# Maxima over partitions taken by a TensorE product instead of GpSimd, and MoE1's input scaled by the maximum of v

## The chip, the cores and the metric

The kernel runs on one NeuronCore of a Trainium2 chip. TensorE (PE) multiplies, VectorE (DVE), ScalarE (ACT) and GpSimd (POOL) work element by element, SyncE (SP) issues the transfers; each runs its own queue in order and waits on semaphores. Results of TensorE land in PSUM, all else lies in SBUF. The metric is the device time of one execution in microseconds.

## The reference

```python
def attn(q, k, v):                       # 4 x 8 heads, 1152 keys, width 64
    q_pool = q.reshape(B, H, S // 2, 2, D).mean(axis=3)        # 576 queries
    scores = (1 / np.sqrt(D)) * q_pool @ k.T
    e = np.exp(scores - scores.max(-1, keepdims=True))
    return (e / (e.sum(-1, keepdims=True) + 1e-9)) @ v

x = attn(q, k, v)                        # heads side by side: 2304 x 512
h = x @ moe_w_in                         # MoE1, 512 -> 2048
x = (h * sigmoid(h)) @ moe_w_out         # 2048 -> 512
a = x @ w1; b = x @ w2                   # MoE2, 512 -> 1024
out = ((a * b) @ w3) @ w_out             # 1024 -> 1024 -> 512
```

The weights of the two MoE layers come as 64-bit floats, q, k and v as 32-bit ones.

## The kernel before, in words

Most products run as three fp16 products. An operand is multiplied by a power of two (the scale), rounded to fp16 (`hi`, by ScalarE) and the remainder is rounded again (`lo`, by VectorE or, for MoE1's `g` and MoE2's product `a*b`, by GpSimd). `hi*hi + hi*lo + lo*hi` are then accumulated in PSUM. The scale comes from the operand's largest absolute value: VectorE reduces along each partition, GpSimd over the partitions (`allmax`, L309 and L310), and `pow2` (L301 to L307, three small VectorE instructions) makes the power of two. Such maxima are taken of each v (12, for the batch entries 1 to 3), of each MoE1 input block (9), of the weight groups (`wst` of w_in and of w_out, `ws` of w1 and w2 together) and of each MoE2 input block (6).

Attention works on a batch entry, a head pair and tiles of 128 queries. A score tile (L465) lies in one of two PSUM tiles `sc`; VectorE takes the row maxima (L502), ScalarE the exponential (L482). In batch entry 0 (`WHOLE`) the exponentials are transposed by TensorE in fp32 (L514, into `sc` as well), evacuated by ScalarE (L517), multiplied with v in fp32 (L555), and the reciprocal row sums are spread over the output by a product with a tile `dg` (L523 writes it, L562 uses it). In entries 1 to 3 they are split to fp16 (L530 and L493), transposed by DMA and multiplied with the split v (L610), and ScalarE evacuates the product with v's scale into `x32` (L620).

MoE1 runs in blocks of 256 tokens: entry b gives blocks 2b (g = 0) and 2b + 1 (g = 1), the left-over queries of all entries block 8 (`x32t`). `block_ops` takes the maximum of `x32` (L632, then GpSimd), the scales (L637 and L638), and the split to `x16` (L656 and L643), all behind the last head pair's product. Then come 8 units of 24 products with w_in (`h_unit`, L676), each with tanh, gate and split behind it, and 16 of 12 products with w_out (`x_unit`, L717). Until the attention is over, the products other than scores and transposes alternate on two PSUM tiles `mm`; later there are eight (`mm` and `mt`).

When the attention's buffers are through, w1, w2, w_out and w3 of MoE2 are loaded and converted (`job`), w1 and w2 are split with the scale of `ws` (`split16`, L886 to L905), and MoE2 multiplies them (L1119), forms w3 times w_out once (`w3o`, L1015, with one buffer `w3t` for its transposed operand) and multiplies by that (L1163).

The order on every queue comes from a planner in the kernel (`Plan.run`): each operation has an engine, a cost in microseconds, the buffers that it reads and writes, and a key. The planner simulates the engines with these costs, and of the operations ready on an engine issues the one with the lowest key. The issued order is fixed in the program. A changed cost or operation therefore moves others.

Of the kernel before, what the change touches and what calls it, by code (L numbers as in the profile page):

```python
# [27 lines left out]
LOAD_AFTER = 3.0  # L28
AFTER = {PE: 0.25, ACT: 0.2, DVE: 0.15, POOL: 0.2, SP: 0.0}
# [35 lines left out]
class Plan:  # L65
# [5 lines left out]
    def op(self, eng, cost, fn, r=(), w=(), key=0.0, land=None):  # L71
# [3 lines left out]
        o.n, o.hook = len(self.ops), None  # L75
# [39 lines left out]
    def run(self):  # L115
        cand = defaultdict(list)
        free = {e: 0.0 for e in ENGINES}
        free["CTL"] = 0.0
        order = []
# [17 lines left out]
        while any(cand.values()):  # L137
# [47 lines left out]
def kernel(  # L185
# [51 lines left out]
    ident_b = Buf(Tag(1))  # L237

# [70 lines left out]
    def allmax(dst, src):  # L309
        nc.gpsimd.partition_all_reduce(dst, src, channels=P, reduce_op=bass_isa.ReduceOp.max)  # L310

    def from_f64(dst, words, dst_b, words_b, key):
# [20 lines left out]
        op(DVE, 1.85, merge, [words_b], [dst_b], key + 0.01)  # L333
# [13 lines left out]

    kts, qts, v16s, mvs = {}, {}, {}, {}
# [14 lines left out]
    def prep_q(b, g, hp):  # L363
# [20 lines left out]
        op(DVE, 0.7 + 0.13 * g, pool, [qs], [qt], i0 - 7)  # L384

    def prep_v(b, hp):
        i0 = FIRST_T[(b, 0, hp)]
        v16, mv = attn_buf(t_v16), attn_buf(t_mv) if b >= WHOLE else None
# [41 lines left out]
        op(DVE, 1.36, top, [vs], [(mv, 0)], i0 - 4)  # L430
        op(POOL, 0.4, lambda: allmax(mv.t[:, 1:2], mv.t[:, 0:1]), [(mv, 0)], [(mv, 1)], i0 - 3.9)
        op(DVE, 0.8, scales, [(mv, 1)], [(mv, 2)], i0 - 2)
        op(ACT, 1.26, hi, [vs, (mv, 2)], [(v16, 0)], i0 - 1)
        op(DVE, 1.45, lo, [vs, (mv, 2), (v16, 0)], [(v16, 1)], i0 + 0.5)
# [11 lines left out]
    def tile_ops(i):  # L446
# [53 lines left out]
        op(PE, 1.14, qk, [kt, qt], [sc], i - 1.5)  # L500
# [4 lines left out]
        op(ACT, 1.43, soft_exp, [sc, (sm, 0)], [e, (sm, 1)], i - 3.0 * whole)  # L505
        op(DVE, 0.32, inverse, [(sm, 1)], [(sm, 2)], i + 0.2)
        if whole:
            st, dg = Buf(t_s), attn_buf(t_dg)
            dgs[i] = dg
# [9 lines left out]
            op(PE, 1.1, turn32, [e, ident_b], [st, (pt, (j % 2, 0))], i + 0.3)  # L519
# [13 lines left out]
        op(DVE, 1.45, lo, [e, (sm, 2), (p16, 0)], [(p16, 1)], i + 0.8)  # L533
        op(SP, 2.75, turn, [p16], [(pt, j % 2)], i + 1, land=5.2)

    def pv_whole(b, g, hp, i, last, ps, nn, mine, x32, off):
# [22 lines left out]
        def spread():  # L559
            for (a, jj), dg in inv.items():  # L560
# [3 lines left out]
                    dg.t,  # L564
# [6 lines left out]
        op(  # L571
            PE, 0.3 if last else 0.6, spread, [ident_b] + [dg for k_, dg in inv.items() if not last or k_ == (0, 0)],
# [3 lines left out]
        op(PE, 1.4 if last else 4.5, pv, [v16] + list(mine.values()), [ps, (x32, (hp, off, 0))], i + 2.5)  # L576
# [8 lines left out]
    def pv_ops(b, g, hp, i, last=False):  # L585

        v16, mv = v16s[(b, hp)], mvs[(b, hp)]
# [30 lines left out]

        def evac():
            nc.scalar.activation(x32.t[:, hp, off : off + nn], ps.t[:, :nn], AF.Copy, scale=mv.t[:, 4:5])  # L620

        op(PE, 1.2 if last else 2.95, pv, [v16] + list(mine.values()), [ps, (x32, (hp, off, 0))], i + 2.5)
        op(ACT, 0.3 if last else 0.45, evac, [ps, (mv, 2)], [(x32, (hp, off))], i - SOON)


    def block_ops(blk, i, span):

        x32, xm = x32s[blk], moe_buf(t_xm)
        x16 = moe_buf(t_x16)
# [4 lines left out]
        def scales():  # L634
            m = xm.t
            pow2(m[:, 1:2], m[:, 2:3], m[:, 3:4])
            nc.vector.tensor_scalar_mul(m[:, 3:4], m[:, 3:4], 0.5)  # L637
            nc.vector.tensor_scalar(  # L638
                m[:, 4:5], m[:, 2:3], wst[0][:, 1:2], 2.0 ** -4, op0=ALU.mult, op1=ALU.mult
            )  # L640
# [165 lines left out]
    for b in range(B):  # L806
        for g in range(2):
            for hp in range(NP):
# [9 lines left out]
                if g:  # L818
                    pv_ops(b, g, hp, i0 + 4, last=True)
# [422 lines left out]
```

## Time and profile before

| | |
|---|---|
| median of 3 runs | 1200.62 us (1199.74 to 1205.22) |
| profiled execution, its own time | 1200.74 us |
| its span, first to last instruction | 1198.7 us |
| TensorE busy | 1108.2 us (92%) |
| VectorE busy | 792.2 us (66%) |
| ScalarE busy | 663.2 us (55%) |
| GpSimd busy | 158.1 us (13%) |
| mean granted TensorE clock | 0.974 |

Busy time counts from an instruction's start to its end. It is an average over stages that differ: the first 250 us hold batch entry 0 and the conversion of MoE1's weights, up to 745 us entries 1 to 3 run with MoE1 in their gaps, up to 857 us the last MoE1 blocks, then MoE2. A wait is put down to the engine whose signal came last; "issue" is time for which the profile shows no wait.

### The profile page before, as it was taken

Reading aid. Unit: us, or ns where it says so; the run is one execution under the profiler, and the core shown is the slowest. Engines: PE = TensorE matmul, PEld = TensorE weight load, DVE = VectorE, ACT = ScalarE, POOL = GpSimd, SP = SyncE. Lnnn points to the kernel's source line nnn. Section 1 sums busy time; section 2 is a strip of 40 time slices with the busy share of each in tenths; the row PEclk is TensorE's granted clock in tenths of the full one; section 3 lists DMA queues with packets and bytes.
Section 4 is the critical chain, followed back from the end, with each engine's and each line's share of the span. In section 5 each row is a group of like instructions: output and inputs, shape, how many; then the busy total and the mean of one; then the engine's idle time right before and its main releaser. Section 6 shows DMA issues by size and latency. Waiting matters only on the chain.

```text
span 1198.7 us, 21922 instructions
## 1 busy us (share of the span) xinstructions
PE 1108.2 (92%) x8972; PEld 809.1 (67%) x8972; DVE 792.2 (66%) x1283; ACT 663.2 (55%) x986; POOL 158.1 (13%) x156
## 2 busy tenths in 40 slices
PE   3778897999999999999899999897999999999998
PEld 2445675767776767677677777786756776767666
DVE  6988898498788788797987785576977521212110
ACT  3656667567677577686686675465634322222221
POOL 0000120012012012020020020112121111111211
PEclk9978998999999999999999999898999999999999
DMA  9635344368988997989979778454334001010001
GB/s 348 211 134 184 115 140 157 115 136 169 181 182 171 218 194 166 190 174 200 199 145 200 151 123 148 147 194 137 124 123 150 1 27 54 12 42 27 10 18 27
DMA packets 294821, 163.17 MB, mean 136 GB/s; under 512 B 256064, under 2 KB 266816, under 8 KB 294720
## 3 DMA queue, kind: packets, MB, share of 16 engines
q1 hardware_dynamic: 294720, 161.77, 55.6%
q8 instruction: 70, 1.15, 0.4%
q14 instruction: 31, 0.25, 0.1%
HBM read 80.22 MB, written 9.44 MB: 75 GB/s over the span
## 4 chain that ended last, share of the span: by engine, by line
PE 51%; DVE 3%; issue 2%; DMA 1%; ACT 1%; POOL 1%; DVEq 0%; POOLq 0%; ACTq 0%
PE mt L1119 10%; PE mm L676 7%; PE mt L1163 6%; PE mm L717 5%; PE sc L465 5%; PE mm L1119 4%; PE mm L610 4%; PE mt L1015 3%; PE mt L676 3%; PE mt L717 2%; PE mm L1163 2%; DMA pt<-p 1%; PE mm L1015 0%; DVE sm L502 0%; DVE x L643 0%
## 5 line engine op out<-in xcount | busy, mean ns | idle before, releaser
L465 PE MATMUL sc<-kt,qt 64*128 64x128 f32 (+3 forms) x960 | 200.7, 534 | 29.0 <-ACT pt L517 20.9
L502 DVE TENSOR_REDUCE sm<-sc 128x1 f32<-128x1152 f32 x144 | 193.9, 1348 | 40.5 <-PE sc L465 40.2
L676 PEld LDWEIGHTS <-w 128*128 128x128 f16 x1728 | 169.7, 100 | 60.6 <-issue 35.9
L482 ACT ACTIVATE e<-sc,sm 128x1152 f32<-128x1152 f32 x144 | 175.2, 1217 | 47.9 <-DVE sm L502 42.8
L717 PEld LDWEIGHTS <-w 128*128 128x128 f16 x1728 | 164.3, 98 | 54.2 <-issue 30.9
L676 PE MATMUL mm<-x,w 128*128 128x256 f16 x1440 | 173.2, 279 | 18.6 <-DVE x L643 9.7
L493 DVE SCALAR_TENSOR_TENSOR p<-e,sm,p 128x1152 f16<-128x1152 f32 x108 | 159.5, 1484 | 29.7 <-ACT p L530 29.2
L717 PE MATMUL mm<-g,w 128*128 128x256 f16 x1440 | 169.8, 273 | 2.8 <-POOL g L701 1.9
L465 PEld LDWEIGHTS sc<-kt,qt 64*128 64x128 f32 (+1 forms) x960 | 91.8, 182 | 97.9 <-issue 57.1
L530 ACT ACTIVATE p<-e,sm 128x1152 f16<-128x1152 f32 x108 | 134.2, 1248 | 31.4 <-DMA pt<-p 10.7
L701 POOL TENSOR_TENSOR g<-t,g 128x512 f16<-128x512 f32 x72 | 94.6, 1319 | 297.8 <-ACT g L698 237.0
L1139 DVE SCALAR_TENSOR_TENSOR abf<-mt,x2m,asb 128x384 f32<-128x384 f32 x36 | 22.1, 615 | 123.9 <-PE mt L1119 123.9
L610 PE MATMUL mm<-pt,v 128*64 128x256 f16 (+1 forms) x1944 | 89.8, 250 | 5.3 <-DMA pt<-p 5.1
L610 PEld LDWEIGHTS <-v 128*64 128x64 f16 x1944 | 81.9, 112 | 13.4 <-DMA pt<-p 6.6
L1119 PEld LDWEIGHTS <-w1h 128*128 128x128 f16 x576 | 56.1, 99 | 41.5 <-issue 6.2
L1119 PEld LDWEIGHTS <-w2h 128*128 128x128 f16 x576 | 56.2, 98 | 38.0 <-issue 1.3
L1119 PE MATMUL mt<-x2h,w2h 128*128 128x384 f16 x432 | 76.1, 326 | 0.0
L1119 PE MATMUL mt<-x2h,w1h 128*128 128x384 f16 x384 | 69.4, 331 | 2.1 <-DVE x2h L1081 1.5
L514 PE MATMUL sc<-identr,e 128*128 128x128 f32 x324 | 50.1, 308 | 17.9 <-ACT e L482 17.8
L692 ACT ACTIVATE t<-mm,xm 128x512 f32<-128x512 f32 x60 | 41.1, 685 | 38.4 <-PE mm L676 35.0
L514 PEld LDWEIGHTS sc<-identr,e 128*128 128x128 f32 x324 | 41.1, 158 | 30.1 <-ACT e L482 25.2
L517 ACT COPY pt<-sc 128x1152 f32<-128x1152 f32 x36 | 40.3, 1118 | 32.1 <-PE sc L514 31.9
(131 smaller groups left out, 1336.1 us busy)
## 6 DMA issues: line engine op xcount, KB each, us to landing
v<-in_moe_w_dram SPq DMA_DIRECT2D x32, 512.0 KB, 4.2
qs<-in_q_dram SPq DMA_DIRECT2D x16, 640.0 KB, 4.8
kt<-in_k_dram SPq DMA_DIRECT2D x16, 576.0 KB, 4.6
qs<-in_q_dram SPq DMA_DIRECT2D x16, 512.0 KB, 4.5
g<-in_moe_w_in_dram SPq DMA_DIRECT2D x16, 512.0 KB, 6.1
w<-t SPq DMA_DIRECT2D x32, 256.0 KB, 3.3
stage<-in_v_dram SPq DMA_DIRECT2D x12, 576.0 KB, 4.6
x2d<-t SPq DMA_DIRECT2D x36, 128.0 KB, 2.3
```

The lines of the kernel that those rows point to most:

```text
L465: nc.tensor.matmul(sc.t[cols, bank, : (c1 - c0) * P], qt.t[rows * D : (rows + 1) * D, 4 if last else 2 * h + j - 2 * g, cols], kt.t[rows * ...
L482: nc.scalar.activation(e.t, flat(), AF.Exp, bias=sm.t[:, 0:1], accum_out=sm.t[:, 1:2])
L493: nc.vector.scalar_tensor_tensor(p16.t[:, 1], e.t, sm.t[:, 3:4], p16.t[:, 0], op0=ALU.mult, op1=ALU.subtract)
L502: DVE, 1.36, lambda: nc.vector.tensor_reduce(sm.t[:, 0:1], flat(), axis=AX.X, op=ALU.max, negate=True),
L514: nc.tensor.transpose(to[:, c * P : (c + 1) * P], e.t[:, c * P : (c + 1) * P], ident)
L530: ACT, 1.27, lambda: nc.scalar.activation(p16.t[:, 0], e.t, AF.Copy, scale=sm.t[:, 3:4]),
L610: nc.tensor.matmul(ps.t[a * D : (a + 1) * D, :nn], v16.t[:, a, KEYS[c], tv, :], rhs, start=idx == 0, stop=idx == 3 * NK - 1,)
L676: nc.tensor.matmul(ps.t[:, f % 2 * BL : (f % 2 + 1) * BL], w16[0][ct * NQ + f // 4][:, tw, (f % 4) * P : (f % 4 + 1) * P], x16.t[:, ct, tx ...
L701: nc.gpsimd.tensor_tensor(gv(1), two(g32), gv(0), op=ALU.subtract)
L717: nc.tensor.matmul(ps.t[:, :BL], w16[1][f][:, tw, ct * P : (ct + 1) * P], gs[u].t[:, f % 4, tg, :], start=f == 0 and n == 0, stop=f == NF ...
L1119: nc.tensor.matmul(ps.t[:, :TB], buf.t[:, ct, tw, f * P : (f + 1) * P], xr.t[:, ct, tx, :], start=idx == 0, stop=idx == 11,)
L1163: nc.tensor.matmul(ps.t, ab[f].t[:, ta, m * P : (m + 1) * P], w3_b.t[:, f, tb, :], start=f == 0 and n == 0, stop=f == NF2 - 1 and n == 2,)
```

## The change

`allmax` is gone. In its place `top_mm` multiplies the column of partial maxima, spread over 128 columns by a zero stride, with the identity: each PSUM row then holds all 128 maxima, and VectorE reduces them. It takes a PSUM tile of the tag `mm`. For entries 1 to 3 the attention's output is bounded by the largest |v| of the entry, so MoE1's scale comes from v's maxima (`vmx`) before the attention is done; `mv` holds all head pairs' scales. The product of probabilities and v is then split straight from PSUM (`x_hi`, `x_lo`): for g = 1 all four head pairs, for g = 0 the last one, while the first three go through `x32` as before and are split together. Blocks 0 and 1 keep the maximum of `x32`; block 8 takes the largest `vmx`, for entry 0 from the maximum of its part of `x32t`. The constant factor in x's scale goes from 0.5 to 8, that in w_in's from 2^2 to 2^-2, so their product stays. `spread` reads the reciprocal sums with a zero stride, so `dg` is not written. The planner's costs are adjusted, a change between fp32 and fp16 products costs it 0.1, and score tiles are tied to the one before and to the transpose three tiles back.

```diff
@@ planner @@
+SWITCH = 0.1
+            late = 0.0
+            if e == PE and o.mode != mode:
+                late, mode = SWITCH, o.mode
@@ maxima over partitions @@
-    def allmax(dst, src):
-        nc.gpsimd.partition_all_reduce(dst, src, channels=P, reduce_op=bass_isa.ReduceOp.max)
+    def top_mm(dst, src, r, w, key):
+        am = Buf(t_mm)
+        op(
+            PE, 0.3,
+            lambda: nc.tensor.matmul(am.t[:, :P], src().to_broadcast([P, P]), ident, start=True, stop=True),
+            [r], [am], key,
+        )
+        op(DVE, 0.22, lambda: nc.vector.reduce_max(dst(), am.t[:, :P], axis=AX.X), [am], [w], key)
@@ prep_v @@
-        op(POOL, 0.4, lambda: allmax(mv.t[:, 1:2], mv.t[:, 0:1]), [(mv, 0)], [(mv, 1)], i0 - 3.9)
+        top_mm(lambda: col(1), lambda: col(0), (mv, (hp, 0)), (mv, (hp, 1)), i0 - 3.9)
+        if hp == NP - 1:
+            xm = xms[2 * b]
+            op(
+                DVE, 0.15, lambda: nc.vector.reduce_max(vmx[:, b : b + 1], mv.t[:, 1, :], axis=AX.X),
+                [(mv, (h_, 1)) for h_ in range(NP)], [(vmx_b, b)], i0 - 1.9,
+            )
+            op(DVE, 0.8, lambda: x_scales(xm, vmx[:, b : b + 1]), [(vmx_b, b), wst_b[0]], [(xm, 2)], i0 - 1.9)
...
@@ tile_ops @@
-        op(PE, 1.14, qk, [kt, qt], [sc], i - 1.5)
+        scores = op(PE, 1.19, qk, [kt, qt], [sc], i - 1.5, mode=1)
+        if i - 3 in turns:
+            plan.link(scores, {turns[i - 3]})
+        if i:
+            plan.link(scores, {asked[i - 1]})
+        asked[i] = scores
...
-            op(
-                DVE, 0.2,
-                lambda: nc.vector.tensor_scalar(
-                    dg.t, ident[:, :D], 0.0, sm.t[:, 3:4], op0=ALU.mult, op1=ALU.add
-                ),
-                [(sm, 2), ident_b], [dg], i + 0.6,
-            )
@@ pv_ops @@
+        straight = b >= WHOLE and not last and (g == 1 or hp == NP - 1)
+        if straight:
+            def x_hi():
+                nc.scalar.activation(x16.t[:, hp, 0], ps.t[:, :nn], AF.Copy, scale=mv.t[:, 5, hp : hp + 1])
+            def x_lo():
+                nc.vector.scalar_tensor_tensor(
+                    x16.t[:, hp, 1], ps.t[:, :nn], mv.t[:, 5, hp : hp + 1], x16.t[:, hp, 0],
+                    op0=ALU.mult, op1=ALU.subtract,
+                )
...
@@ block_ops @@
-        op(DVE, 1.25, top, [x32], [(xm, 0)], i - 6)
-        op(POOL, 0.4, lambda: allmax(xm.t[:, 1:2], xm.t[:, 0:1]), [(xm, 0)], [(xm, 1)], i - 6)
+        elif not bound:
+            op(DVE, 1.25, top, [x32], [(xm, 0)], i - 6)
+            top_mm(lambda: xm.t[:, 1:2], lambda: xm.t[:, 0:1], (xm, 0), (xm, 1), i - 6)
...
@@ split16, of w1 and w2 @@
-        op(POOL, 0.4, lambda: allmax(ws2[:, 4:5], ws2[:, 0:1]), [ws2_b], [ws2_b], key)
+        top_mm(lambda: ws2[:, 4:5], lambda: ws2[:, 0:1], ws2_b, ws2_b, key)
```

The order of instructions at three places follows. First GpSimd's queue in MoE1's block 8, before the change. `g` are the gated values whose low parts GpSimd subtracts, `ws` the maximum of w1 and w2, `x2m` that of MoE2's first block.

```order
L701 TENSOR_TENSOR g_177<-t_3_187,g_177 128x2x256
L701 TENSOR_TENSOR g_177<-t_1_185,g_177 128x2x256
L701 TENSOR_TENSOR g_178<-t_0_184,g_178 128x2x256
L310 ISA
L310 ISA ws_192<-ws_192 128x1
L701 ISA
L701 TENSOR_TENSOR g_178<-t_2_186,g_178 128x2x256
L701 TENSOR_TENSOR g_179<-t_1_185,g_179 128x2x256
L701 TENSOR_TENSOR g_179<-t_0_184,g_179 128x2x256
L701 TENSOR_TENSOR g_180<-t_4_188,g_180 128x2x256
L701 TENSOR_TENSOR g_180<-t_1_185,g_180 128x2x256
```

The same units of block 8 on GpSimd after the change:

```order
L766 TENSOR_TENSOR g_174<-t_2_183,g_174 128x2x256
L766 TENSOR_TENSOR g_174<-t_3_184,g_174 128x2x256
L766 TENSOR_TENSOR g_175<-t_1_182,g_175 128x2x256
L766 TENSOR_TENSOR g_175<-t_2_183,g_175 128x2x256
L766 TENSOR_TENSOR g_176<-t_3_184,g_176 128x2x256
L766 TENSOR_TENSOR g_176<-t_1_182,g_176 128x2x256
L766 TENSOR_TENSOR g_177<-t_4_185,g_177 128x2x256
L766 TENSOR_TENSOR g_177<-t_0_181,g_177 128x2x256
```

The instructions without operands and the all-reduce between the subtractions are gone; the subtractions follow one another.

Second, TensorE's queue in the same block, at the end of the fifth unit (products with w_in tiles `w_0`), before:

```order
L676 MATMUL mm_82<-x_1_182,w_0_14_159 128x256
L676 LDWEIGHTS w_0_14_159
L676 MATMUL mm_82<-x_1_182,w_0_14_159 128x256
L676 LDWEIGHTS w_0_2_147
L676 MATMUL mm_83<-x_1_182,w_0_2_147 128x256
L676 LDWEIGHTS w_0_2_147
```

and after, where the product of `ws` with the identity stands ahead of the sixth unit:

```order
L741 MATMUL mm_84<-x_1_179,w_0_14_156 128x256
L741 LDWEIGHTS w_0_14_156
L741 MATMUL mm_84<-x_1_179,w_0_14_156 128x256
L320 MATMUL mm_83<-identr,ws_189 128x128
L741 LDWEIGHTS w_0_2_144
L741 MATMUL mt_7786<-x_1_179,w_0_2_144 128x256
```

TensorE now has in its own queue, between two units, an instruction that needs `ws` from VectorE.

Third, VectorE's queue from the last split of probabilities (`p`) to the input of block 7 (`x_0`), before, with the maxima and the scales (`xm`) of blocks 7 and 8:

```order
L493 SCALAR_TENSOR_TENSOR p_2_111<-e_108,sm_124,p_2_111 128x1152
L632 TENSOR_REDUCE xm_190<-x_0_115 128x1
L632 TENSOR_REDUCE xm_191<-x32t_116 128x1
L303 TENSOR_SCALAR xm_190<-xm_190 128x1
L304 TENSOR_SCALAR xm_190<-xm_190 128x1
L307 TENSOR_SCALAR xm_190<-xm_190 128x1
L637 TENSOR_SCALAR xm_190<-xm_190 128x1
L638 TENSOR_SCALAR xm_190<-xm_190,wst_72 128x1
```

After these come seven small ones and the two splits L643 of 1024 columns, for blocks 7 and 8. The whole place after the change:

```order
L533 TENSOR_SCALAR sm_129<-sm_129 128x1
L536 RECIPROCAL sm_129<-sm_129 128x1
L539 SCALAR_TENSOR_TENSOR p_1_111<-e_108,sm_127,p_1_111 128x1152
L539 SCALAR_TENSOR_TENSOR p_2_112<-e_109,sm_129,p_2_112 128x1152
L673 SCALAR_TENSOR_TENSOR x_0_178<-mm_84,mv_130,x_0_178 128x256
L705 SCALAR_TENSOR_TENSOR x_1_179<-x32t_117,xm_188,x_1_179 128x4x256
L760 SCALAR_TENSOR_TENSOR t_4_185<-t_0_181,mm_84 128x512
```

The maxima and the scales have left the place, and of block 7's split one head pair is left.

## Rows read from the trace of the kernel before

**Rows 1.** busy time of each engine in stretches of the span, us
```profile
30.00:205.00 175.00, 144.98 (x1035) 97.66 (x1034) 158.31 (x313) 115.72 (x168) 12.95 (x15) 0.89 0.47 158
...
253.00:745.00 492.00, 474.07 (x4811) 358.18 (x4811) 401.07 (x586) 351.74 (x483) 70.98 (x60) 0.99 0.89 175
745.00:857.00 112.00, 95.70 (x896) 83.51 (x894) 76.51 (x123) 62.92 (x120) 21.27 (x20) 0.94 0.47 143
857.00:1199.00 342.00, 334.54 (x1780) 229.40 (x1778) 109.33 (x176) 95.33 (x165) 51.54 (x53) 0.99 0.16 51
```

**Rows 2.** TensorE's waits over the span: us in total, times, longest
```profile
PE sc L465 <- ACT pt L517: 20.9, 17, 2.0
...
PE mt L717 <- POOL g L701: 9.6, 2, 8.9
...
PE mm L717 <- POOL g L701: 1.9, 1, 1.9
PE mt L1119 <- DVE x2h L1081: 1.5, 1, 1.5
```

**Rows 3.** TensorE's waits for the split input from 300 to 770 us
```profile
PE mm L676 <- ACT x L656: 7.9, 5, 3.5
PE mm L676 <- DVE x L643: 7.3, 6, 1.9
```

**Rows 4.** order of time at block 7's start: start, us, what [idle before]
```profile
754.27 0.47 ACT L620 ACTIVATE x<-mm,mv 128x256 f32<-128x256 f32 x1 [6.40 <-PE mm L610]
...
757.72 1.15 ACT L656 ACTIVATE x<-x,xm 128x1024 f16<-128x1024 f32 x1 [1.97 <-DVE xm L637]
...
758.90 1.28 DVE L643 SCALAR_TENSOR_TENSOR x<-x,xm,x 128x1024 f16<-128x1024 f32 x1 [0.15 <-ACT x L656]
758.91 0.27 PE L676 MATMUL mm<-x,w 128*128 128x256 f16 x1 [3.53 <-ACT x L656]
...
760.23 6.95 PE L676 MATMUL mm<-x,w 128*128 128x256 f16 x47 [1.05 <-DVE x L643]
```

**Rows 5.** order of time on TensorE, first units of blocks 5 and 6
```profile
595.85 4.34 PE L676 MATMUL mm<-x,w 128*128 128x256 f16 x23 [1.14 <-DVE x L643]
...
674.67 2.67 PE L676 MATMUL mm<-x,w 128*128 128x256 f16 x23 [0.76 <-DVE x L643]
```

**Rows 6.** order of time around the maximum of w1 and w2
```profile
826.18 0.38 POOL L310 PARTITION_ALL_REDUCE ws<-ws  x1 [6.15 <-issue]
...
834.59 2.26 POOL L701 TENSOR_TENSOR g<-t,g 128x512 f16<-128x512 f32 x2 [8.04 <-issue]
...
835.79 5.76 PE L717 MATMUL mt<-g,w 128*128 128x256 f16 x36 [8.89 <-POOL g L701]
```

**Rows 7.** order of time before it: first loads, TensorE's unit 4, last partial maximum
```profile
761.51 1.76 SPq L918 DMA_DIRECT2D v<-in_moe_w_dram  x4
...
814.18 5.40 PE L676 MATMUL mm<-x,w 128*128 128x256 f16 x48
...
817.25 0.19 ACT L929 ACTIVATION_READ_ACCUMULATOR wfb<-w 128x1 f32 x1
```

**Rows 8.** line L514, transposes: duration in ns, least, median, most
```profile
L514 PEld LDWEIGHTS sc<-identr,e x324: 137/142/231, 13.2 to 236.4; 128*128 128x128 f32 x162
L514 PE MATMUL sc<-identr,e x324: 272/273/476, 13.2 to 236.5; 128*128 128x128 f32 x162
```

**Rows 9.** VectorE's groups of instructions by line: busy us, mean ns, idle before
```profile
L760 DVE TENSOR_REDUCE wmx<-w 128x1 f32<-128x512 f32 x32 | 21.8, 680 | 0.5
...
L632 DVE TENSOR_REDUCE xm<-x 128x1 f32<-128x1024 f32 x8 | 9.7, 1215 | 8.9 <-ACT x L620 8.7
L523 DVE TENSOR_SCALAR dg<-identr,sm 128x64 f32<-128x64 f32 x36 | 8.7, 249 | 5.7 <-PE mm L562 5.5
...
L767 DVE TENSOR_REDUCE wst<-wmx 128x1 f32<-128x16 f32 x2 | 0.3, 164 | 0.0
```

**Rows 10.** busy time of each engine from 861 to 892 us
```profile
861.00:892.00 31.00, 31.00 (x186) 19.48 (x185) 27.97 (x41) 12.81 (x24) 6.17 (x5) 1.00 0.50 164
```

More of the change, by code (lines that the diff above doesn't have):

```diff
@@ L152, in run @@
             o.start = at
+            late = 0.0
+            if e == PE and o.mode != mode:
+                late, mode = SWITCH, o.mode
             if e != "CTL":
-                free[e] = at + o.cost
-            o.end = at + (o.cost if o.land is None else o.land)
+                free[e] = at + o.cost + late
+            o.end = at + (o.cost if o.land is None else o.land) + late
             order.append(o)
@@ L570, in pv_whole @@
         sp, rs = Buf(t_mm), attn_buf(t_rs)
-        op(
-            PE, 0.3 if last else 0.6, spread, [ident_b] + [dg for k_, dg in inv.items() if not last or k_ == (0, 0)],
+        first = op(
+            PE, 0.3 if last else 0.6, spread, [ident_b] + [(dg, 2) for k_, dg in inv.items() if not last or k_ == (0, 0)],
             [sp, (rs, 0)], i + 1.0,
@@ L575, in pv_whole @@
         op(ACT, 0.3 if last else 0.45, lambda: nc.scalar.copy(rs.t[:, :nn], sp.t[:, :nn]), [sp], [(rs, 1)], i - SOON)
-        op(PE, 1.4 if last else 4.5, pv, [v16] + list(mine.values()), [ps, (x32, (hp, off, 0))], i + 2.5)
+        pv_op = op(PE, 1.1 if last else 4.4, pv, [v16] + list(mine.values()), [ps, (x32, (hp, off, 0))], i + 2.5, mode=2)
+        plan.link(pv_op, {first})
         op(
@@ L619, in evac @@
         def evac():
-            nc.scalar.activation(x32.t[:, hp, off : off + nn], ps.t[:, :nn], AF.Copy, scale=mv.t[:, 4:5])
-        op(PE, 1.2 if last else 2.95, pv, [v16] + list(mine.values()), [ps, (x32, (hp, off, 0))], i + 2.5)
-        op(ACT, 0.3 if last else 0.45, evac, [ps, (mv, 2)], [(x32, (hp, off))], i - SOON)
+            nc.scalar.activation(x32.t[:, hp, off : off + nn], ps.t[:, :nn], AF.Copy, scale=mv.t[:, 4, hp : hp + 1])
+        op(PE, 0.85 if last else 2.95, pv, [v16] + list(mine.values()), [ps, (x32, (hp, off, 0))], i + 2.5, mode=2)
@@ L626, in block_ops, with hi @@
+        op(ACT, 0.3 if last else 0.45, evac, [ps, (mv, (hp, 2))], [(x32, (hp, off))], i - SOON)
     def block_ops(blk, i, span):
-        x32, xm = x32s[blk], moe_buf(t_xm)
-        x16 = moe_buf(t_x16)
+        b, g = divmod(blk, 2)
+        bound = WHOLE <= b < B
+        x32, xm = x32s.get(blk), xms[blk]
+        x16 = x16s[blk]
+        n_ = NP - 1 if bound else NP
         def top():
             nc.vector.reduce_max(xm.t[:, 0:1], x32.t, axis=AX.XY, apply_absolute_value=True)
[L634 to L640, printed above, removed]
+        def hi():
+            nc.scalar.activation(x16.t[:, :n_, 0], x32.t[:, :n_], AF.Copy, scale=xm.t[:, 3:4])
@@ L662, in block_ops @@
+        if not (bound and g):
+            got = [(x32, (h_, 0)) for h_ in range(n_)] if bound else [x32]
+            to = [[(x16, (h_, t)) for h_ in range(n_)] for t in range(2)]
+            op(ACT, 0.15 + 0.25 * n_, hi, got + [(xm, 2)], to[0], i - 6)
+            op(DVE, 0.15 + 0.27 * n_, lo, got + [(xm, 2)] + to[0], to[1], i - 6)
         units = NF // 2 + 4 * NC
```

139 lines of the change are left out of this document (90 added, 49 removed).

## The prediction

> **What bounds the kernel now.** I read four views. First the busy time by stretches [rows 1]: from 253 to 745 us (attention of the batch entries 1 to 3 with MoE1 in its gaps) TensorE is busy 474.07 of 492 us, and from 857 us to the end (MoE2) 334.54 of 342, so there a microsecond taken from TensorE's waits is a microsecond of the end. In the first entry (30 to 205 us) it is busy only 144.98 of 175 at a mean clock of 0.89, while VectorE is busy 158.31: VectorE paces that stage. From 745 to 857 TensorE is busy 95.70 of 112 although nothing else is full: something makes it wait.
>
> Second, TensorE's waits [rows 2, 3] say what. In the first entry it waits above all for ScalarE's evacuations of transposed tiles (20.9 us). From 300 to 770 us it waits 7.9 + 7.3 = 15.2 us for `x` of L656 and L643, the split MoE1 input, at the starts of blocks 2 to 7. It also waits 9.6 + 1.9 = 11.5 us for GpSimd's low part of `g` (L701).
>
> Third, the order of time at such a start [rows 4]: block 7's input is complete at 754.74 us, its maximum is reduced by VectorE, then by GpSimd, turned into a scale by five small VectorE instructions, split by ScalarE (1.15) and by VectorE (1.28, begun 758.90). TensorE, with no scores left to fill the gap, stands 3.53 us and then 1.05. A long gap costs again behind it: block 5's first unit needed 4.34 us for 23 products, block 6's 2.67 [rows 5], which is half the granted clock, 1.2 instead of 2.4 GHz, over 1.7 us of lost time.
>
> Fourth, GpSimd at 826 us [rows 6]: the all-reduce itself takes 0.38 us, but GpSimd waits for nothing on the profile for 6.15 us before it and for 8.04 us behind it, before the next subtraction of `g`. In the order rows, instructions without operands stand at just these two places: GpSimd changes its code. TensorE stands 8.89 us for it and then runs 36 products in 5.76 us, where 48 take 5.40 at full clock [rows 7], so 5.76 - 36/48 x 5.40 = 1.7 us more.
>
> **The change part by part, against the profiled run's 1200.74 us** (its span is 1198.7, what lies around it 2.0; the median of the runs shown is 1200.62, so both bases agree).
>
> 1. *Starts of blocks 2 to 7.* With the scale known from v, the last head pair's product goes from PSUM into `x` by one ScalarE and one VectorE instruction of 256 columns (the like-sized evacuation L620 takes 0.47 [rows 4]), instead of evacuation, maximum, all-reduce, scale and two splits. TensorE has a score tile or a MoE product to run meanwhile at blocks 2 to 6, at block 7 the tail's product. Of 15.2 us I take off 14; the bounds are 8 and 15.2. Of the half-clock losses behind the starts of blocks 3, 5 and 7 (4.34 - 2.67 = 1.7 us, three times) I take off 4, bounds 0 and 5.
>
> 2. *GpSimd's code changes.* No all-reduce is left, so no change of code after the start: off go 11.5 us of TensorE's wait and the 1.7 us of clock, -13.2. Both ends of this are firm, as the subtractions then follow ScalarE directly.
>
> 3. *What is late next there.* The maximum over w1 and w2 is now a product in TensorE's own queue, behind unit 4 of block 8, and the rest of MoE1 is queued behind it. Its last partial maximum came at 817.25 + 0.19 = 817.44 us, from weights whose loads began at 761.51, when the attention's buffers were through [rows 7]. With block 8's input split without the chain, those loads start about 3 us earlier (x's last split would begin some 3 us sooner than in rows 4), so about 814.3. TensorE finished unit 4 at 814.18 + 2.7 = 816.9, half of the 48 products begun there [rows 7]; without block 7's wait (3.53 + 1.05 = 4.6) and clock loss (1.7) it is there at 810.6. So a new wait of 814.3 - 810.6, about 4 us: +4, bounds 0 (the loads gain as much as TensorE) and 8 (VectorE, whose queue holds the reduction, is late as well).
>
> 4. *The products' price.* 24 products of a column against the identity. The nearest row is the 128x128 fp32 transposes: weights 0.14 us, matmul 0.27 in the median and 0.48 at most [rows 8]. Hidden weights and pipelining give 0.14 as the low end, the slowest row 0.48; I take 0.3. Nine fall in the first entry's stage, which TensorE does not pace; 15 do count: +4.5, bounds 2 and 7. VectorE's reduction of each lies between 0.164 (16 columns) and 0.680 (512 columns) [rows 9], by the line between them 0.28, 24 times 6.7 us; it loses seven of nine maxima at 1.2 us (8.5) and 36 `dg` at 0.249 (9.0), so it has more room, not less. Each product also holds one of two PSUM tiles that the MoE units alternate on, for that reduction; score tiles, which use other PSUM, stand beside most products in the new order, so I cost it at nothing; without that cover it is one wait of up to 1 us for each of the 8 in the middle stage.
>
> 5. *First entry.* `dg` goes: 36 x 0.249 = 9.0 us of VectorE, and 5.5 us in which VectorE stood until TensorE released a `dg` buffer [rows 9]. At best the stage shortens by 14.5; at worst by nothing, as ScalarE's evacuations also end waits there [rows 2]. The scores are now tied to the transpose three tiles before; nothing in the profile prices that. I take half, -7.
>
> 6. *MoE2's beginning.* The wait of 1.5 us for `x2h` (L1081), which came behind a code change, goes [rows 2]; but the first two W3 products now stand with only the small product between them, and their one transposed operand buffer must be refilled meanwhile by four instructions of 512 columns, 0.68 us each by the nearest row [rows 9], 2.7 in a line and about 2 where ScalarE's and VectorE's overlap: +0.5 on balance, bounds -1.5 and +2.7.
>
> Sum: -14 - 4 - 13.2 + 4 + 4.5 - 7 + 0.5 = -29.2, so 1171.5; forecast **1172**.
>
> **Rivals.**
>
> *The tail gives its gain back.* From 861 to 892 us VectorE is busy 27.97 of 31 us and TensorE 31.00 [rows 10]. If TensorE arrives at MoE2 about 14 us earlier while VectorE's conversion of the weights does not, the first W3 products wait. Then block 7's start (4.6), its clock (1.7) and the GpSimd stall's 9.6 + 1.7 are lost again, less the new wait already counted (4): +13.6, so about 1186. For it: VectorE is nearly full there. Against it: from 745 to 857 us VectorE is busy only 76.51 of 112 [rows 1], part of that idleness came from the same stall, and the conversion would use it.
>
> *Slower: TensorE becomes the one that waits for maxima.* GpSimd is busy 70.98 of 492 us in the middle stage [rows 1] and could stand in its queue before each v maximum; TensorE cannot. If each of the 15 products on the path waits for the VectorE reduction before it, which itself stands behind one wide maximum and one wide split, that is 1.22 + 1.28 = 2.5 us each by the nearest rows [rows 4, 9], 37.5 us: 1172 + 37 = 1209. It decides from 29.2 / 15 = 1.9 us a product on. Against it: in the new order the v maxima of entries 2 and 3 are reduced tens of VectorE instructions ahead of most of their products; only one or two stand within ten. The Trainium skill ("GPSIMD Engine Reference", Engine selection) gives a reduction along partitions to GpSimd, which is the rule that speaks against this change. Here a row has 0.38 us for the reduction and 6.15 + 8.04 = 14.2 us of standing around it [rows 6], so the trace doesn't bear the rule out where the code must be changed.
>
> *No difference.* The starts' waits are replaced one for one: the direct splits hold a PSUM tile until VectorE, with two wide instructions ahead, has read it, and the first entry stays bound by ScalarE. Then only the GpSimd stall goes, against the products and the new wait: -13.2 + 4 + 4.5 + 0.5 = -4.2, about 1197.
>
> **How the numbers follow.** Forecast 0.68, tail rival 0.14, no difference 0.09, slower 0.09. The forecast's own bounds: best -15.2 - 5 - 13.2 + 0 + 2 - 14.5 - 1.5 = -47.4, so 1153; worst -8 - 0 - 13.2 + 8 + 7 - 0 + 2.7 = -3.5, so 1197; all bad ends together are unlikely, and the range of 8 in 10 is 1153 to 1194, which takes in the tail rival. Half a per cent, 6 us, is what a measurement of this kernel can tell from no change: faster is below 1194.6. Faster: the forecast but for 0.02, and the tail rival, and a little of the third, 0.82; same 0.10; slower 0.08.
>
> **What would show it.** After: no idle of 6 us or more on GpSimd that ends in nothing shown; no wait of TensorE for GpSimd's `g`; waits for `x` at blocks 2 to 7 under 2 us in sum; a wait of some microseconds before the product on `ws`, where I put 4; VectorE's `dg` rows gone and the first entry's last block-0 product some 7 us earlier; MoE2 as long as before. The forecast is wrong if waits at the 24 products (or for PSUM tiles behind them) exceed 10 us, if the first W3 products wait over 8 us, or if the first entry doesn't shorten.

## The result and the profile after

| | before | after |
|---|---|---|
| median | 1202.19 us (1199.74 to 1205.22, 4 runs) | 1167.12 us (1166.58 to 1168.36, 4 runs) |
| ratio | | 0.9709, 95% interval 0.9682 to 0.9735 |
| span of the profiled execution | 1198.7 us | 1164.8 us |

The forecast was 1172, between 1153 and 1194, faster with a chance of 0.82. The time came out 35 us under before, 5 us under the forecast.

Busy time by stretches, cut at the same events in both kernels (start, first unit of MoE1's block 1, first MoE2 product, end); first the kernel before. Columns: stretch, length, busy time of PE, PEld, DVE, ACT, POOL, granted clock, DMA share, GB/s.

```profile
0.00:253.30 253.30, 203.96 (x1491) 138.01 (x1492) 205.62 (x402) 153.49 (x220) 14.34 (x23) 0.93 0.51 172
253.30:857.25 603.95, 569.99 (x5706) 441.88 (x5706) 477.53 (x708) 414.51 (x603) 92.25 (x80) 0.98 0.81 169
857.25:1198.70 341.45, 334.29 (x1778) 229.18 (x1775) 109.08 (x175) 95.18 (x165) 51.54 (x53) 0.99 0.16 51
```

The same view of the kernel after:

```profile
0.00:252.40 252.40, 199.94 (x1514) 137.69 (x1515) 204.03 (x374) 155.26 (x223) 10.65 (x14) 0.91 0.53 175
252.40:825.02 572.62, 562.45 (x5721) 439.72 (x5721) 469.12 (x719) 410.60 (x598) 86.91 (x64) 1.00 0.89 179
825.02:1164.80 339.78, 333.96 (x1788) 230.10 (x1785) 107.49 (x175) 94.88 (x163) 50.08 (x48) 1.00 0.15 49
```

Nearly all of it lies in the middle: 603.95 to 572.62, 31.3 us. There TensorE's idle time fell from 34.0 to 10.2 us (length minus busy), and its busy time by 7.5 although it has ten products more, with a granted clock of 1.00 instead of 0.98 (by these two digits 0.02 x 604, about 12 us of lost clock, an estimate). The first stretch ends 0.9 us earlier, MoE2 is 1.7 us shorter.

The forecast had it otherwise: -22.7 us by its terms 1 to 4, nearly all of it in the middle, and -7 in the first entry.

TensorE's waits over the span after (us in total, times, longest):

```profile
PE sc L565 <- ACT e L528: 17.9, 5, 10.9
PE sc L511 <- ACT pt L568: 16.5, 13, 1.8
...
PE mm L658 <- DMA pt<-p: 6.0, 6, 1.8
...
PE mt L320 <- DVE x2m L1165: 2.8, 1, 2.8
...
PE mm L741 <- DVE vmx L323: 1.4, 1, 1.4
...
PE mm L741 <- DVE x L673: 0.2, 1, 0.2
```

Of the 15.2 us for `x` [rows 3] 0.2 are left, of the 11.5 for GpSimd's `g` [rows 2] nothing. The waits of the first entry are there as before. New is a wait of 2.8 us for `x2m`, the maximum of MoE2's first block.

Block 7's start after, in order of time (start, us, what [idle before]):

```profile
736.37 0.47 ACT L670 ACTIVATE x<-mm,mv 128x256 f16<-128x256 f32 x1 [4.18 <-PE mm L658]
736.88 0.48 DVE L673 SCALAR_TENSOR_TENSOR x<-mm,mv,x 128x256 f16<-128x256 f32 x1 [9.08 <-ACT x L670]
...
737.41 2.78 PE L741 MATMUL mm<-x,w 128*128 128x256 f16 x24 [0.23 <-DVE x L673]
```

Two instructions of 256 columns stand where TensorE waited 4.6 us for a chain [rows 4], and the unit behind runs at the full clock, 2.78 for 24 products.

The maximum of `ws` after, in order of time:

```profile
789.80 0.17 DVE L964 TENSOR_REDUCE ws<-wmx 128x1 f32<-128x16 f32 x1 [0.19 <-ACT wfb L1007]
789.81 2.78 PE L741 MATMUL mm<-x,w 128*128 128x256 f16 x24
...
792.43 0.39 PE L320 MATMUL mm<-identr,ws 128*128 128x128 f32 x2
```

The last partial maximum came about 28 us earlier than before (817.44, [rows 7]), while TensorE came to this place 24 us earlier. So the product found its operand there and waited for nothing. GpSimd's line after names no wait but that for ScalarE (busy, mean ns | idle before):

```profile
L766 POOL TENSOR_TENSOR g<-t,g 128x512 f16<-128x512 f32 x72 | 96.9, 1346 | 709.9 <-ACT g L763 709.9
```

### The profile page after: what moved, and what is told of

It is laid out like the page before. It is cut to its first block, busy times and chain, and to the rows that moved or that the text cites. A ratio compares the mean times of both kernels' runs of the same rounds, so it can differ in the third digit from the quotient of the medians.

```text
span 1164.8 us, 21847 instructions
## 1 busy us (share of the span) xinstructions
PE 1096.4 (94%) x9020; PEld 807.5 (69%) x9020; DVE 780.6 (67%) x1266; ACT 660.7 (57%) x983; POOL 147.6 (13%) x126
## 5 line engine op out<-in xcount | busy, mean ns | idle before, releaser
L511 PE MATMUL sc<-kt,qt 64*128 64x128 f32 (+3 forms) x960 | 197.0, 527 | 27.4 <-ACT pt L568 16.5
L782 PEld LDWEIGHTS <-w 128*128 128x128 f16 x1728 | 163.8, 98 | 42.1 <-issue 18.8
L741 PEld LDWEIGHTS <-w 128*128 128x128 f16 x1728 | 165.5, 98 | 39.5 <-issue 18.5
L782 PE MATMUL mm<-g,w 128*128 128x256 f16 x1536 | 180.4, 273 | 1.7 <-DMA w<-t 1.7
L741 PE MATMUL mm<-x,w 128*128 128x256 f16 x1416 | 163.7, 273 | 4.3 <-DVE t L760 1.8
L574 ACT ACTIVATE p<-e,sm 128x1152 f16<-128x1152 f32 x108 | 134.4, 1249 | 37.9 <-DMA pt<-p 11.8
L1217 DVE SCALAR_TENSOR_TENSOR abf<-mt,x2m,asb 128x384 f32<-128x384 f32 x37 | 22.7, 615 | 120.2 <-PE mt L1197 119.1
L658 PEld LDWEIGHTS <-v 128*64 128x64 f16 x1944 | 80.9, 111 | 13.2 <-DMA pt<-p 6.3
L1197 PE MATMUL mt<-x2h,w1h 128*128 128x384 f16 x456 | 80.4, 326 | 0.0
L565 PE MATMUL sc<-identr,e 128*128 128x128 f32 x324 | 47.7, 300 | 17.9 <-ACT e L528 17.9
L568 ACT COPY pt<-sc 128x1152 f32<-128x1152 f32 x36 | 40.0, 1116 | 26.3 <-PE sc L565 26.3
```

What stands on the lines that cost most here:

```text
L511: nc.tensor.matmul(sc.t[cols, bank, : (c1 - c0) * P], qt.t[rows * D : (rows + 1) * D, 4 if last else 2 * h + j - 2 * g, cols], kt.t[rows * ...
L565: nc.tensor.transpose(to[:, c * P : (c + 1) * P], e.t[:, c * P : (c + 1) * P], ident)
L574: ACT, 1.27, lambda: nc.scalar.activation(p16.t[:, 0], e.t, AF.Copy, scale=sm.t[:, 3:4]),
L658: nc.tensor.matmul(ps.t[a * D : (a + 1) * D, :nn], v16.t[:, a, KEYS[c], tv, :], rhs, start=idx == 0, stop=idx == 3 * NK - 1,)
L741: nc.tensor.matmul(ps.t[:, f % 2 * BL : (f % 2 + 1) * BL], w16[0][ct * NQ + f // 4][:, tw, (f % 4) * P : (f % 4 + 1) * P], x16.t[:, ct, tx ...
L782: nc.tensor.matmul(ps.t[:, :BL], w16[1][f][:, tw, ct * P : (ct + 1) * P], gs[u].t[:, f % 4, tg, :], start=f == 0 and n == 0, stop=f == NF ...
```

## The experiments

Ratios are to the kernel before on the same chip. Except where it is said, an edit is made to the kernel after, whose ratio is 0.9709 (0.9682 to 0.9735); line numbers then shift by up to ten. The kernel after has one measurement of 4 runs, so a difference to it can hold a difference of chips. The intervals of dg_back, old_plan, no_links, code_change, twice, thin_wmx and thin_evac overlap with its own: what such a run shows lies in its trace.

| run | edit | median us | ratio (95%) |
|---|---|---|---|
| pool_max | maxima back on GpSimd | 1185.29 | 0.9866 (0.9834 to 0.9899) |
| x_max | x bounded by its own maximum | 1193.45 | 0.9934 (0.9914 to 0.9954) |
| both_back | both | 1190.61 | 0.9899 (0.9864 to 0.9934) |
| no_dg | before, without `dg` | 1192.29 | 0.9925 (0.9899 to 0.9952) |
| dg_back | `dg` written again | 1170.29 | 0.9737 (0.9722 to 0.9752) |
| old_plan | planner undone | 1169.50 | 0.9731 (0.9715 to 0.9747) |
| no_links | links of score tiles out | 1166.90 | 0.9705 (0.9674 to 0.9736) |
| code_change | one all-reduce put back | 1174.46 | 0.9762 (0.9713 to 0.9812) |
| twice | every product twice | 1163.25 | 0.9675 (0.9627 to 0.9722) |
| thin_wmx | weight maxima of 32 columns | 1158.61 | 0.9638 (0.9590 to 0.9687) |
| thin_evac | half the evacuations' columns | 1168.08 | 0.9722 (0.9664 to 0.9780) |
| sum_bound | weights bounded by a sum | 1144.93 | 0.9532 (0.9493 to 0.9572) |

**pool_max.**

```diff
     def top_mm(dst, src, r, w, key):
-        am = Buf(t_mm)
-        op(PE, 0.3, ...)
-        op(DVE, 0.22, ...)
+        op(POOL, 0.4, lambda: nc.gpsimd.partition_all_reduce(dst(), src(), ...), [r], [w], key)
```

> All maxima over partitions go back to GpSimd's all-reduce, everything else stays as after the change (v still bounds MoE1's input, the planner and the links stay). Theory (two separate gains): GpSimd's changes of code return at ws, so TensorE waits again for g near the end of MoE1 (11.5 us and about 1.7 of clock in the profile before), while the 15 products that lie on TensorE's path go (0.4 us each by the rows after, 6 us): 1167 + 13.2 - 6 = 1174, between 1171 and 1180, and the starts of blocks 2 to 7 stay without a wait for x. Rival A (the products made the whole gain): 1190 to 1200. Rival B (the products cost what they save): 1163 to 1169.

Measured: 18 us more than after; the theory's 7 was too little. The stretch from block 1's first unit to MoE2 is 12.3 us longer than after (584.9 us), MoE2 4.1 us, where TensorE waits 5.3 us for `x2h`. TensorE's waits from 250 to 860 us:

```profile
PE mm L779 <- POOL g L763: 11.1, 3, 7.0
PE mt L779 <- POOL g L763: 5.4, 2, 4.0
...
PE mm L738 <- DVE x L670: 0.2, 1, 0.2
```

The starts stay free of waits, as said. But GpSimd's changes of code now stop TensorE in the middle stage too, at maxima of v; one of them on GpSimd, in order of time:

```profile
294.93 0.38 POOL L318 PARTITION_ALL_REDUCE mv<-mv  x1 [6.25 <-DVE sm L533]
303.50 1.14 POOL L763 TENSOR_TENSOR g<-t,g 128x512 f16<-128x512 f32 x1 [8.20 <-issue]
```

and TensorE there:

```profile
304.70 1.23 PE L779 MATMUL mm<-g,w 128*128 128x256 f16 x5 [6.98 <-POOL g L763]
```

**x_max.**

```diff
-        straight = b >= WHOLE and not last and (g == 1 or hp == NP - 1)
+        straight = False
-        bound = WHOLE <= b < B
+        bound = False
...
```

> MoE1's input is again bounded by its own maximum: all nine blocks take the maximum of x32, reduced by the product with the identity, and are split from x32 in one piece; v's maximum is used for v alone. The rest is as after the change. Theory (the waits at the starts of blocks 2 to 7 hang on the chain of evacuation, maximum, scale and two splits, not on GpSimd's part of it): most of the 18 us forecast for the starts (14 of idle and 4 of clock) is lost again, 1167 + 14 = 1181, between 1176 and 1187, with TensorE's waits for x of 8 us or more in sum. Rival (the all-reduce on GpSimd was the slow part of the chain, so the product alone shortens the starts): 1167 to 1173, waits for x under 5 us.

Measured: 26 us more than after, more than the theory, and by another way than it said. TensorE's waits from 250 to 860 us begin with

```profile
PE sc L511 <- ACT e L528: 10.3, 8, 3.0
PE mm L658 <- DMA pt<-p: 5.8, 5, 2.1
PE mm L741 <- DVE x L705: 2.7, 3, 1.4
```

The waits for `x` are small (the last row above and one of 1.6 us for L702): putting the chain back did not bring back the 15.2 us of before, so the theory falls. Of what was lost, 7.6 us went into waits of score tiles for exponentials, at 250 to 265 us, where MoE1's block 1 was not ready to fill the gaps (its first unit began at 272 instead of 252 us). The order was planned anew, so how much is the chain and how much the order stays open.

**both_back.** The two edits together.

> Both parts undone together, with the planner, the links and the spread without dg left as after the change: maxima on GpSimd and MoE1's input bounded by its own maximum. Alone they cost 18 us (GpSimd) and 26 us (own maximum), 44 together, while the whole change is worth 35. Theory (the two overlap: a start that waits for the chain gives GpSimd time to change its code beside it): 1196 to 1203, which leaves the rest of the change (planner, links, dg) at 0 to 6 us. Rival (they add up, and the rest of the change costs time): 1208 to 1214.

Measured: below both theories. TensorE's waits from 250 to 860 us:

```profile
PE mt L779 <- POOL g L763: 8.9, 1, 8.9
PE mm L738 <- DVE x L702: 5.9, 6, 1.4
PE mm L738 <- ACT x L699: 3.8, 1, 3.8
...
PE mm L779 <- POOL g L763: 0.2, 1, 0.2
```

The waits for `x` and the one long GpSimd stall of the kernel before are back (9.7 and 8.9 us), but the stalls in the middle stage, 11.1 us in pool_max, are 0.2 here. In these orders the product alone gave nothing (1190.6 to 1193.5), v's bound alone 5.3 us (the intervals overlap in both cases), the two together 23.5, clear of noise. That GpSimd's code changes lay beside the starts' waits fits these rows, but the order differs too, so it is not shown.

**no_dg.** The kernel before with one edit.

```diff
-                lambda: nc.vector.tensor_scalar(dg.t, ident[:, :D], 0.0, sm.t[:, 3:4], ...),
...
-                    dg.t,
+                    dg.t[:, 3:4].to_broadcast([P, D]),
```

> The kernel before with one edit alone: dg is not written, and the spread products read the reciprocal sums with a zero stride (sm with twelve buffers, as after the change). Everything else is the kernel before: GpSimd's maxima, own maximum of x, old planner. The forecast's term 5 by itself: 1201 - 7 = 1194. With both other parts undone the rest of the change was worth 10 to 12 us; if dg is all of it: 1189 to 1192. If most of that is the planner's: 1196 to 1200. Rival (the waits in the middle stage take the gain back): 1199 to 1202.

Measured: 10 us off, between 6 and 12 by the interval. Its stretches, cut as those of before and after, and then those of both_back:

```profile
0.00:243.24 243.24, 197.07 (x1491) 135.40 (x1491) 199.04 (x370) 152.72 (x220) 16.61 (x23) 0.96 0.51 177
243.24:846.70 603.46, 570.38 (x5707) 442.08 (x5707) 472.84 (x704) 414.62 (x603) 96.87 (x80) 0.98 0.81 170
846.70:1187.50 340.80, 332.62 (x1778) 228.63 (x1776) 108.99 (x175) 95.17 (x165) 51.54 (x53) 1.00 0.15 51
```

```profile
0.00:255.02 255.02, 199.30 (x1491) 138.53 (x1491) 198.99 (x370) 152.27 (x220) 13.71 (x23) 0.92 0.49 169
255.02:844.80 589.78, 566.18 (x5708) 439.28 (x5708) 475.48 (x703) 413.52 (x602) 97.41 (x80) 0.99 0.83 174
844.80:1189.50 344.70, 335.25 (x1778) 229.46 (x1775) 110.20 (x176) 95.36 (x165) 51.78 (x53) 0.99 0.15 51
```

Against before the first stretch is 10.1 us shorter and the others stay within 0.7, so the edit to `dg`, with the order planned anew, did in the first entry what term 5 said. Of the 10.1 us 6.9 are TensorE's busy time, at a mean clock of 0.96 instead of 0.93; only 3.2 are idle time. both_back differs from this kernel by the planner's part (and the buffers of v's scales) and takes nearly the same time, but by another way: 11.8 us more in the first stretch, 13.7 less in the middle, 3.9 more in MoE2. The new planner gives away in the first entry what `dg` gained there, and wins it back in the middle.

**dg_back.** The reverse of it in the kernel after.

> dg is written again by VectorE (36 instructions of about 0.25 us in the first entry, with its four buffers, and sm with its eight) and the spread products read it. The rest is as after the change. Theory from the two traces (VectorE does not pace the first entry, so dg was beside other work): 1167 to 1169. The forecast's own step (half of 14.5 us): 1174, with block 1's first unit 7 us later.

Measured: 3.2 us more. The reduction that ends entry 0 (`vmx`, L323 after) is a milestone for the first entry. In the kernel after, then here (times: first and last start):

```profile
L323 DVE TENSOR_REDUCE vmx<-mm x1: 282/282/282, 252.1 to 252.1; 128x1 f32<-128x128 f32 x1
```

```profile
L324 DVE TENSOR_REDUCE vmx<-mm x1: 280/280/280, 257.6 to 257.6; 128x1 f32<-128x128 f32 x1
```

The same line in code_change, whose first entry is that of the kernel after (its edit lies far behind):

```profile
L323 DVE TENSOR_REDUCE vmx<-mm x1: 281/281/281, 254.8 to 254.8; 128x1 f32<-128x128 f32 x1
```

So this milestone moves by 2.7 us between two traces of one order; of the 5.5 us that the first entry lost here, between 2.8 and 5.5 may be the work for `dg`. The middle is 2 us shorter than after (570.6 us), where TensorE's waits for DMA transposes are 2.9 instead of 6.0 us; in traces of the order of after they are 3.6 to 6.0 (0.4 in twice).

**old_plan and no_links.**

```diff
-SWITCH = 0.1
+SWITCH = 0.0
-        if i - 3 in turns:
-            plan.link(scores, {turns[i - 3]})
-        if i:
-            plan.link(scores, {asked[i - 1]})
...
```

no_links takes out the four lines on links alone.

> The planner's part of the change is undone: no cost for a change between fp32 and fp16 products, the old costs, and no links of the score tiles to the one before and to the transpose three back (nor of the product with v to its spread). The products and v's bound stay. Theory (that part is worth little, the forecast counted nothing for it): 1167 within 4 us either way, 1163 to 1171. Rival (a good part of the gain is the planner's, above all in the first entry): 1175 or more, with the first unit of block 1 over 5 us later than at 252.4 us.

> Only the links of the score tiles (to the one before and to the transpose three back) are taken out; the costs stay, and the order is planned anew. Theory (the links slow the first entry, where the run with the old planner was 4 to 6 us earlier, and the costs serve the rest): 1161 to 1165. Rival (the links and the costs only work together): 1167 to 1171.

Measured: 2.4 us more, and the same as after. The planner's part is worth 0 to 3 us in the end, and the theory for no_links falls: without the links entry 0 ends at 253.0 us, no earlier than after. With the old planner it ends at 246.9, 5.2 earlier, and the middle loses it again (580.1 us against 572.6). That is the same exchange as between no_dg and both_back.

**code_change.**

```diff
                 nc.gpsimd.tensor_tensor(gv(1), two(g32), gv(0), op=ALU.subtract)
+                if blk == 2 * B and u == 4:
+                    nc.gpsimd.partition_all_reduce(wst[0][:, 3:4], wst[0][:, 0:1], ...)
```

> One all-reduce of a column that nothing reads is put back on GpSimd, behind the subtraction of the fifth unit of block 8; the order on every engine is otherwise as after the change, and nothing waits for its result. Theory (GpSimd changes its code before and behind it, 6.15 and 8.04 us before the change): the subtraction of the sixth unit begins at about 812 instead of 801 us, TensorE, which wants it at 803.2, waits 10 us, 2.8 of which were a wait anyway: 1167 + 7.5, with the clock behind it up to 9.2, 1174 to 1177. Rival (the all-reduce costs its 0.4 us, the stall before the change came from ws being late): 1167 to 1168.

Measured: 7.3 us more, as the theory said. In the traces 2.7 of it lie in the first entry, which the edit does not touch; the middle is 5.6 us longer (578.2 us), which is about the stall below less the 2.8 us of the wait for `x2m` that it replaces. GpSimd in this run:

```profile
797.93 1.16 POOL L766 TENSOR_TENSOR g<-t,g 128x512 f16<-128x512 f32 x1 [2.61 <-ACT g L763]
804.62 0.90 POOL L768 PARTITION_ALL_REDUCE wst<-wst  x1 [5.53 <-ACT t L757]
812.60 3.37 POOL L766 TENSOR_TENSOR g<-t,g 128x512 f16<-128x512 f32 x3 [7.08 <-issue]
```

and TensorE:

```profile
813.79 6.41 PE L786 MATMUL mt<-g,w 128*128 128x256 f16 x41 [8.22 <-POOL g L766]
```

The operand was there since the first entry, so the 5.53 us before the all-reduce are no wait for data, whatever the row names as releaser. The instructions without operands show in the trace by name, here right behind the subtraction that ends at 799.09:

```profile
L768 POOLq MODIFY_POOL_CONFIG  x2: 12/12/12, 799.0 to 799.1; - x2
```

In the kernel before the partial maxima had been reduced when GpSimd came free there, at 820.03, 6.15 us before its all-reduce:

```profile
819.52 0.16 DVE L886 TENSOR_REDUCE ws<-wmx 128x1 f32<-128x16 f32 x1
```

So the stall of the kernel before was the change of code, not a late `ws`: that rival falls.

**twice.**

```diff
-            lambda: nc.tensor.matmul(am.t[:, :P], src().to_broadcast([P, P]), ident, start=True, stop=True),
+            lambda: [nc.tensor.matmul(am.t[:, :P], ..., ident, start=True, stop=True) for _ in range(2)],
```

> Each of the 24 products with the identity runs twice, into the same PSUM tile; the order on every engine stays as after the change. Forecast: 0.3 us each for the 15 on TensorE's path, 1167 + 4.5 = 1171.6; by the rows after, where one product takes 0.39 to 0.46 us with its two weight loads, 1167 + 6 = 1173. Rival A (they lie in TensorE's gaps): 1167 to 1168. Rival B (the slower rival of the forecast, a wait behind each): over 1180.

Measured: 3.9 us less by the medians, with intervals that overlap; no theory said so. A product's row after, and the same one here:

```profile
389.94 0.39 PE L320 MATMUL mm<-identr,mv 128*128 128x128 f32 x2
```

```profile
385.59 0.61 PE L320 MATMUL mm<-identr,mv 128*128 128x128 f32 x4
```

The second copy adds 0.22 us, so the price is between 0.22 and the 0.38 to 0.49 of a whole one, near the 0.3 of the forecast. The total is hidden by two other things: entry 0 ends 2.3 us earlier, where the mean clock from 30 to 120 us was 0.92 instead of 0.84, and the waits for DMA transposes are 0.4 instead of 6.0 us. The first is no more than two traces of one order differ (2.7 us between after and code_change, which ended later at a clock of 0.87), so it need not come from the edit or the clock; for the second no cause is shown. For the time of the whole the run is inconclusive; it rules out the rival of long waits behind each product.

**thin_wmx and thin_evac.** What paces the first entry?

```diff
-                    wmx[wi][:, c : c + 1], whole[c], axis=AX.X, ...
+                    wmx[wi][:, c : c + 1], whole[c][:, :32], axis=AX.X, ...
```

```diff
-                nc.scalar.copy(pt32(pt)[:, j % 2], st.t...[:, :S])
+                nc.scalar.copy(pt32(pt)[:, j % 2, : S if i < 8 else S // 2], st.t...[:, : S if i < 8 else S // 2])
```

> The 32 maxima of the converted MoE1 weights read 32 of their 512 columns (this leaves out most of that maximum); the order on every engine stays as after the change. This takes about 32 x (0.68 - 0.2) = 15 us of VectorE out of the first 120 us. The forecast's reading (VectorE paces the first entry): 1152 to 1160. Theory from the trace after (VectorE's work there lies beside a ring of two score tiles in PSUM, through which scores, exponentials, transposes and evacuations pass in turn): 1164 to 1167.

> From the ninth score tile of the first entry on, ScalarE evacuates 576 of the 1152 transposed columns (the rest of the tile is left as it was, so part of the computation is left out); the order on every engine stays as after the change. 28 evacuations become about 0.6 us shorter, 17 us of ScalarE, and each PSUM tile comes free 0.6 us earlier. Theory (the ring of two score tiles paces the first entry): 5 to 15 us faster, 1152 to 1162. Rival (VectorE paces it): 1165 to 1167.

Measured: 8.5 us less, and 1.0 more, which is no change. The end of entry 0 (252.1 after) in thin_wmx, then in thin_evac:

```profile
L323 DVE TENSOR_REDUCE vmx<-mm x1: 280/280/280, 246.0 to 246.0; 128x1 f32<-128x128 f32 x1
```

```profile
L323 DVE TENSOR_REDUCE vmx<-mm x1: 281/281/281, 251.0 to 251.0; 128x1 f32<-128x128 f32 x1
```

My theory of the two PSUM tiles falls: 28 evacuations of 634 instead of 1116 ns on average, 13 us of ScalarE, bring 1.1 us there, less than the 2.7 by which two traces of one order differ. 16 us less of VectorE (32 maxima of 180 instead of 680 ns) bring 6.1. The two runs were timed on the same chip, at the same mean clock from 30 to 120 us (0.91), and differ by 9.5 us in the median and 5.0 at this line. VectorE paces the stage in part, as the forecast read it.

**sum_bound**, drawn from that.

```diff
-                DVE, 0.69,
-                lambda c=c: nc.vector.reduce_max(wmx[wi][:, c : c + 1], whole[c], ...),
+                ACT, 0.9,
+                lambda c=c, junk=junk: nc.scalar.activation(junk.t, whole[c], AF.Abs, accum_out=wmx[wi][:, c : c + 1]),
...
-            [xs], [(xm, 0)], early + 1,
+            [xs], [(xm, 0)], early + 1, land=1.75 if bk else 5.0,
```

> An attempt to beat both kernels: MoE1's weights are bounded by the sum of their absolute values along each partition, which ScalarE accumulates (about 0.9 us each), instead of VectorE's 32 maxima (0.68 us each); the constant factors are shifted to match. The reduction of MoE2's first input is also given a later landing in the planner, so that its product is issued later. The order is planned anew. Theory (VectorE paces the first entry in part and ScalarE doesn't: 16 us less of VectorE gave 8.5 us, 17 us less of ScalarE gave none): 1157 to 1162, without TensorE's wait of 2.8 us for that product. Rival (ScalarE's 29 us more are paid in the same stage): 1167 or more.

Measured: 1144.9, 22 us under after and 56 under before on the same chip, more than the theory. Entry 0 ends at

```profile
L323 DVE TENSOR_REDUCE vmx<-mm x1: 282/282/282, 232.2 to 232.2; 128x1 f32<-128x128 f32 x1
```

19.9 us earlier, which the 16 us of VectorE do not explain at the rate of thin_wmx (6.1): the rest came with the new order and was not taken apart. The wait of 2.8 us for `x2m` is gone. The bound is looser than the maximum, so the split weights use less of the fp16 range.

## Why the prediction was right

*Term 1, the starts (-14 of idle, -4 of clock).* The waits went as forecast: 15.0 us of those for `x`, and the middle ran at the full clock, which gave more than the 4 + 1.7 us counted (TensorE's busy time there fell by 7.5 us with ten products more). What v's bound is worth by itself is less clear: taken back alone (x_max) it costs 26 us, but in other waits than the term named.

*Term 2, GpSimd's code changes (-13.2).* The mechanism is shown: the waits are gone, and one all-reduce put back costs 7.3 us, 5.6 of them in the stretch in which it stands. But the term counted only the stall that the trace of before showed. With the starts' chain gone, GpSimd's other maxima would have cost waits of 11.1 us more in the middle (pool_max).

*Term 3, the new wait for `ws` (+4).* Mis-sized: 0. The loads gained 28 us, TensorE 24; the term's lower bound was the case. A wait of 2.8 us came instead at the product for `x2m`, which the forecast did not name.

*Term 4, the products (+4.5).* The size is confirmed, 0.22 to 0.49 each, and VectorE's reduction takes 0.285 us where 0.28 was read off a line between two rows. No wait for a PSUM tile or a reduction of more than 2.8 us stands behind any of them, so the slower rival's price of 2.5 us each is refuted.

*Term 5, the first entry (-7).* As a saving of `dg` it holds: 10 us in the kernel before, 2.8 to 5.5 us of the first entry in the kernel after, on both sides of the 7. As a forecast of the stage it failed: block 1 begins only 0.9 us earlier in the change as a whole, and a first entry that does not shorten was one of the forecast's own signs of being wrong. The term noted the new ties of the scores and put the planner at nothing. The runs show that the planner's part costs 11.8 us in the first entry and wins 13.7 us in the middle (no_dg to both_back), or 5.2 and 7.5 (old_plan to after).

*Term 6, MoE2's beginning (+0.5).* -1.7 over all of MoE2: the wait for `x2h` went, those for `w3t` are 1.5 us.

*The sum.* By parts it holds: `dg` made -10.0 against -7, the planner's part -1.7 against nothing, the two main parts together, against both_back, -23.5 against the -22.2 of terms 1 to 4 and 6. By stages it does not: the middle gave 31.3 us instead of some 23, the first entry 0.9 instead of 7. That the total is within 5 us of the forecast rests on the planner's losses and gains cancelling, for which the working had no reason; to that extent it is luck. Nor do the two main parts add up one by one: -5.3 and +2.8 alone. The working treated each wait as a price of its own, and the total came out because the change does both. *Rivals:* the tail did not give its gain back (MoE2 is not longer), no start's wait was replaced by another; the third rival's other half, a first entry that keeps its length, did come, though not because ScalarE bounds it (thin_evac).

## What to carry to other kernels

When two waits lie in one stretch, removing one may give little: with v's bound alone the waits for GpSimd's `g` grew from 9.1 (both_back) to 16.5 us (pool_max). Test both together before dropping either. When the order is planned anew, compare stage by stage: a total that stays the same can hide 12 us lost in one stage and won in the next. GpSimd's alternation between an all-reduce and element-wise work cost 12.6 to 14.5 us of standing per pair of changes in the rows shown, also with the operand long there; a product of 0.4 us and a reduction of 0.28 replace it. Where an engine paces a stage in part, try to move its work to one for which a run with less work showed no change (sum_bound).

## What the runs showed of the hardware

A product of a column with the identity in fp32 has two MATMUL records, 0.38 to 0.49 us in all; a second one right behind it adds 0.22. An all-reduce with its operand long there begins 5.53 us after the instruction before it on GpSimd, and the next subtraction 7.08 us after it. MODIFY_POOL_CONFIG stands in the trace at the start of those 5.53 us, not at their end. Taking 13 us of ScalarE's work out of the first entry gave nothing, 16 us of VectorE's 8.5. Two traces with the same instructions in the first entry (after, code_change) had a granted clock from 30 to 120 us of 0.84 and 0.87 and ended that entry 2.7 us apart, so a difference of that size in one trace shows nothing.
